# Fused sparse attention and MoE: the gate row through DRAM, ranks late in the pair, and four weight loads issued later

## The chip, the cores and the metric

The kernel runs on one core of one Trainium2 chip. The metric is the time of one execution on the device in microseconds (us). The kernel before takes 290.99 us, the median of three runs (290.3 to 291.02). Five engines work side by side, each through its own list of instructions in order: PE (TensorE, matrix products), DVE (VectorE), ACT (ScalarE), POOL (GpSimd) and SP (SyncE, which here only issues DMAs). They wait for each other through semaphores. POOL also issues DMAs, those of the weights and all indirect ones.

## The reference

The first half is attention with 4 batches, 8 heads, 768 positions and head size 64. Per query the keys' 24 chunks of 32 are bounded, the six best causal chunks are kept, and the softmax runs over those. Its output, written as 3072 rows x of 512, goes to a mixture of 8 experts with a capacity of 80:

```python
logits = x @ w_gate
expert_idx = np.argmax(logits, axis=1)
gate_w = probs[np.arange(N), expert_idx]          # probs: softmax of the logits
for e in range(E):
    tok_idx = np.where(expert_idx == e)[0]
    if len(tok_idx) > capacity:
        keep = np.argpartition(-gate_w[tok_idx], capacity)[:capacity]
        tok_idx = tok_idx[keep]
    h = np.maximum(x[tok_idx] @ w1[e], 0.0)
    out[tok_idx] = gate_w[tok_idx, None] * (h @ w2[e])
```

An expert keeps its 80 tokens with the largest gate weight; all other rows of the output are zero. So each token's rank inside its expert is needed before the experts can start.

## The kernel before, in words

**Attention.** The loop `for i in range(NP)` (L930) runs over 16 pairs of heads, four to a batch (`kk = i % 4` is the place in the batch). A pair does on PE, in order: scores of steps 0 and 1 (L509, with the chunk mask added by L524), the sums of the pair before (L581, L595), scores of steps 2 and 3, the transposes of the pair before's output rows (L641), scores of steps 4 and 5, the bounds of the next pair (L472), the values (L568), and the transposes of the next pair's unselected chunks (L497). ACT takes the exponentials (L531). POOL makes the causal selects on the diagonal blocks (L545) and adds the exponentials up into ES (the folds, L554), from which the sums are taken. DVE transposes q and k (L439, L449), reduces k to chunk minima and maxima (L453, L454) and picks the six best (L486).

**Ranking a batch.** While batch b is ranked, the pairs of batch b + 1 run (`bb = i // 4 - 1`). At kk = 0 the gate weights of 768 tokens are formed as `gt6`, 128 partitions by 6 tiles (`gate`, L678). They are also needed as a row on all partitions (`G`, columns S to 2S): `rank_row` (L713) makes it with six PE transposes and an ACT copy, and `rank_pred` (L720) writes a slightly smaller copy beside it, with which later tokens lose ties. Then 0/1 matrices are made that tell whose weight beats whose: `rank_own` and `rank_diag` for the diagonal blocks, and `rank_cmp` (L737), one compare of 640 columns for each of six tiles, rotated so that a tile's own block is left out. They lie in the space of weights that come later: tiles 0 to 4 in `w1s[7]`, tile 5 in `w2s[6]` (`Cs`, L303), and the program guards each of these two places as a whole, under the keys `w1_7` and `w2_6` (`Ck`). At kk = 2 `rank_count` (L783) sums them up per expert on PE, and `rank_slot`, `rank_hot`, `table` and `merge` place the tokens in their experts' lists. The last batch is ranked after the loop, by functions of its own (`last_row`, `last_diag`, `last_low`, `last_high`, `last_count`).

**Weights.** `wload(e, part)` (L414) issues from POOL one expert's W1 or W2, 1 MB each, one a pair in pairs 1 to 13; the last three follow in pair 15 (two before its selects). W1 of expert 6 has lent its space as the source of zeros for three of the four fills of the output. W2 of expert 7 has no place of its own: its eight quarters of 128 rows go into spaces that attention has left, with `last_w2` (L919), four in pair 15, and two each behind gathers 4 and 5 of the expert stage.

**Experts.** `gather(e)` (L1088) fetches 80 rows of x by index, `turn(e)` transposes them, `up(e)` multiplies by W1 and takes the relu (half on ACT, L1121, half on DVE, L1123), `down(r)` multiplies four groups of 32 tokens by W2, and a scatter (L1142) writes the rows out. Gathers, scatters and the late W2 loads stand in one order on POOL.

**Order.** There is no scheduler. Each engine's order is that of the program text. The class `Sync` (L18) puts the waits in: for each instruction the names it reads and writes are given, and it waits for the last writer of each, and a writer also for the last readers. A name given as read or written is waited for whether or not the bytes overlap.

Of the kernel before, what the change touches and what calls it, by code (L numbers as in the profile page):

```python
# [4 lines left out]
ALU = mybir.AluOpType  # L5
# [142 lines left out]
def bass_quest_chunk_select__then__topk_capacity_drop_kernel(  # L148
# [57 lines left out]
    with ExitStack() as pers:  # L206
# [13 lines left out]

        sy = Sync(nc)
        op = sy.op

        with nc.Block() as blk:

            @blk.sync
            def _body(_unused):
# [41 lines left out]
                gt6 = al(pers, "gt6", [128, NT])  # L269
# [40 lines left out]

                def T1v(b):
                    return bass.AP(w2s[E - 2], 0, [[FB * Dm, 128], [1, 2 * S]]).bitcast(F32)
# [77 lines left out]
                op("dve", lambda: ve.memset(wg[:], 0.0), w=["wg"])  # L390
                op("dve", lambda: ve.memset(onc[:], 0.0), w=["onc"])
# [286 lines left out]
                def gate(b):  # L678
                    op("dve", lambda: ve.scalar_tensor_tensor(oh[:], lg[:], 0.0, rank_c[:], ALU.is_ge, ALU.mult),
                       r=["lg", "rank_c"], w=["oh"])  # L680
                    op("dve", lambda: ve.tensor_reduce(lmax[:], oh[:], AX, ALU.max), r=["oh", "lmax"], w=["lmax"])
                    op("dve", lambda: ve.tensor_reduce(lsum[:], lgx[:], AX, ALU.add), r=["lgx", "lge"], w=["lsum"])
                    op("dve", lambda: ve.reciprocal(gt6[:], lsum[:]), r=["lsum"], w=["gt6"])
                    op("dve", lambda: ve.tensor_tensor(ohb[:, :, 0:E], oh[:], along(lmax), ALU.is_equal), r=["oh", "lmax"], w=["ohb"])

                def gate_digits(b):
                    op("dve", lambda: ve.tensor_copy(gsp[:, :, 0], gt6[:]), r=["gt6"], w=["gsp0"])
                    op("dve", lambda: ve.tensor_tensor(gdf[:], gt6[:], gsp[:, :, 0], ALU.subtract), r=["gt6", "gsp0"], w=["gdf"])
                    op("dve", lambda: ve.tensor_copy(gsp[:, :, 1], gdf[:]), r=["gdf"], w=["gsp1"])
                    op("dve", lambda: ve.tensor_tensor(gsp[:, :, 2], gdf[:], gsp[:, :, 1], ALU.subtract), r=["gdf", "gsp1"], w=["gsp2"])  # L690
# [11 lines left out]
                PRED = 1.0 - 2.0 ** -24  # L702

                def last_row():
                    for t in range(NT):
                        o = t * 128 if t < 3 else 128 + t * 128
                        gb = bass.AP(gt6, t, [[NT, 128], [0, 128]])
# [5 lines left out]
                def rank_row(b):  # L713
                    for t in range(NT):
                        gb = bass.AP(gt6, t, [[NT, 128], [0, 128]])
                        op("pe", lambda: pe.transpose(SC[1][:, ts(t)], gb, ident_f[:]),
                           r=["gt6", "ident_f"], w=["SC1"], inc=(t == NT - 1))
                    op("act", lambda: ac.activation(G[:, S:2 * S], SC[1][:, 0:S], ACTF.Copy), r=["SC1"], w=["grow"])

                def rank_pred():  # L720
                    op("act", lambda: ac.activation(G[:, 0:S], G[:, S:2 * S], ACTF.Copy, scale=PRED), r=["grow"], w=["growP"])

                def rank_own(b):
                    tq = bass.AP(triQ, 0, [[128, 128], [0, NT], [1, 128]])
                    gb = bass.AP(gt6, 0, [[NT, 128], [1, NT], [0, 128]])
                    op("dve", lambda: ve.tensor_tensor(T1v(b).rearrange("p (a b) -> p a b", a=NT), tq, gb, ALU.mult),
                       r=["triQ", "gt6"], w=["T1"] + Ck(b, NT - 1))

                def rank_diag(b):
                    for j0, n in ((NT - 1, 1), (0, NT - 1)):  # L730
                        o = Cs(b, j0, n, 0, 128)
                        a = T1v(b)[:, j0 * 128:(j0 + n) * 128].rearrange("p (a b) -> p a b", a=n)
                        g = G[:, S + j0 * 128:S + (j0 + n) * 128].rearrange("p (a b) -> p a b", a=n)
                        op("dve", lambda: ve.tensor_tensor(o, a, g, ALU.is_ge), r=["T1", "grow"] + Ck(b, NT - 1),
                           w=[f"D{jt}" for jt in range(j0, j0 + n)] + Ck(b, j0))

                def rank_cmp(b, *jts):  # L737
                    for jt in jts:
                        gj = gt6[:, jt:jt + 1]
                        o = Cs(b, jt, 1, 128, S - 128)[:, 0, :].rearrange("p (a b) -> p a b", a=NT - 1)  # L740
                        op("dve", lambda: ve.tensor_scalar(o, G[:, (jt + 1) * 128:(jt + 1) * 128 + S - 128], gj, None, ALU.is_lt),
                           r=["grow", "gt6"] + (["growP"] if jt < NT - 1 else []), w=[f"C{jt}"] + Ck(b, jt))

                def Cl(jt, lo, w):
                    t, o, row = (ES, jt, 2 * S) if jt < 4 else (vn[0], jt - 4, S)
                    return bass.AP(t, o * (S // 2), [[row, 128], [1, S // 2]]).bitcast(BF16)[:, lo:lo + w]

# [3 lines left out]
                def last_diag(*jts):  # L751
                    for jt in jts:
                        op("dve", lambda: ve.scalar_tensor_tensor(Cl(jt, jt * 128, 128), triQ[:], gt6[:, jt:jt + 1],
                                                                  G[:, S + jt * 128:S + (jt + 1) * 128], ALU.mult, ALU.is_ge),
                           r=["triQ", "gt6"] + gk(jt * 128, jt * 128 + 128), w=[f"D{jt}"])

                def last_low(jt, e):
                    n = jt * 128
                    o, x = Cl(jt, 0, n), G[:, S:S + n]
                    if e == "dve":  # L760
                        op("dve", lambda: ve.tensor_scalar(o, x, gt6[:, jt:jt + 1], None, ALU.is_lt), r=["gt6"] + gk(0, n), w=[f"L{jt}"])
# [4 lines left out]
                def last_high(jt):  # L766
                    n = (jt + 1) * 128
                    op("dve", lambda: ve.tensor_scalar(Cl(jt, n, S - n), G[:, S + n:2 * S], gt6[:, jt:jt + 1], None, ALU.is_le),
                       r=["gt6"] + gk(n, S), w=[f"U{jt}"])

                def last_count(order, warmth):
                    for n, jt in enumerate(order):
                        Cv = Cl(jt, 0, S).rearrange("p (t c i) -> p t c i", c=4, i=32)
                        for c in range(4):
                            op("pe", lambda: pe.matmul(MBf[c * 32:c * 32 + 32, 0:192], ohb[:, jt, :], Cv[:, :, c, :],
                                                       start=(n == 0), stop=(n == NT - 1)),
                               r=["ohb", f"D{jt}"] + ([f"L{jt}"] if jt else []) + ([f"U{jt}"] if jt < NT - 1 else []),
                               w=["MB"], inc=(n == NT - 1 and c == 3))
                        keep_warm(warmth[n])

                ORDER = [5, 4, 3, 2, 1, 0]

                def rank_count(b):  # L783
                    for n, jt in enumerate(ORDER):
                        for lo, hi, o in ((0, NT - jt, jt), (NT - jt, NT, 0)):
                            if lo == hi:
                                continue
                            Cv = Cs(b, jt, 1, lo * 128, (hi - lo) * 128)[:, 0, :].rearrange("p (t c i) -> p t c i", c=4, i=32)
                            last = jt == ORDER[-1]
                            for c in range(4):  # L790
                                op("pe", lambda: pe.matmul(MBf[c * 32:c * 32 + 32, o * 32:(o + hi - lo) * 32], ohb[:, jt, :], Cv[:, :, c, :],
                                                           start=(n == 0 and lo == 0), stop=last),
                                   r=["ohb", f"C{jt}", f"D{jt}"] + Ck(b, jt), w=["MB"], inc=(last and c == 3))
# [136 lines left out]
                for i in range(NP):  # L930
# [10 lines left out]
                    if i == NP - 1:  # L941
                        wload(E - 2, 1)
# [6 lines left out]
                    if live and kk == 1:  # L949
                        rank_pred()  # L950
                        rank_cmp(bb, 5)
# [6 lines left out]
                    if live and kk == 2:  # L958
                        rank_count(bb)
# [15 lines left out]
                    if live and kk == 0:  # L975
                        gate_exp()
                        gate(bb)
                    scores(i, 4, 6)
# [9 lines left out]
                    if i == 3:  # L988
                        op("dve", lambda: ve.tensor_scalar(triM[:], triQ[:], 1.0, 3e38, ALU.is_ge, ALU.mult), r=["triQ"], w=["triM"])
                        op("dve", lambda: ve.scalar_tensor_tensor(triM[:], ident_f[:], 3e38, triM[:], ALU.mult, ALU.max),  # L990
                           r=["triM", "ident_f"], w=["triM"])
                    if i + 4 < NP:
                        load(i + 4, "qk")
                    if i == NP - 4:
                        load_vk(NP - 1, 0)
                    if live and kk == 0:
                        rank_own(bb)
                    if live and kk == 1:
                        rank_diag(bb)
                        rank_cmp(bb, 4, 3, 2, 1, 0)  # L1000
# [17 lines left out]
                    if live and kk == 0:  # L1018
                        rank_row(bb)
# [3 lines left out]
                    if 0 < i < NP - 2:  # L1023
                        wload((i - 1) // 2, (i - 1) % 2)
                    if i in (0, 1, 12):
# [20 lines left out]
                last_high(0)  # L1046
                last_low(5, "act")
                values_out(1)
                last_low(4, "act")
                last_low(3, "act")  # L1050
                last_diag(0, 1, 2, 3, 4, 5)
                last_low(1, "dve")
                last_high(1)
                rows(NP - 1)
                keep_warm(4)
                last_high(4)
                last_high(3)
                last_low(2, "dve")
                last_high(2)
                scale_rows(NP - 1)  # L1060
                gate_gcols(b)
                last_count((0, 5, 1, 4, 2, 3), (0, 0, 0, 0, 0, 6))
# [96 lines left out]
                last_w2((4, 5))  # L1159
                for e in range(1, E):  # L1160
                    if 1 < e + 1 < E:
                        turn(e + 1)
                        if e + 4 < E:
                            gather(e + 4)
                            if e == 1:
                                last_w2((6, 7))
# [41 lines left out]
```

## Time and profile before

The page shows one profiled execution. It took 292.94 us itself, of which the span from the first to the last instruction is 291.1 us.

| | us | share of the span |
|---|---|---|
| PE busy | 275.7 | 95% |
| POOL busy | 226.5 | 78% |
| DVE busy | 213.7 | 73% |
| ACT busy | 147.0 | 51% |
| fold adds on POOL, L554, 135 of them | 148.3 | 51% |
| compares of 640 columns, L741, 18 of them | 15.5 | 5% |
| gate-row transposes on PE, L716, 18 of them | 2.5 | 1% |
| mean granted TensorE clock | 0.988 of full | |

Busy times overlap, as the engines run side by side. The chain of waits, followed back from the last instruction, is 65% PE, 19% POOL and 7% DVE. A pair has no marker of its own; its start can be read from the five transposes L497 and the first score matmul L509 behind them. Loop bodies of one kind recur 16 times with nearly the same durations, so that a pair which differs stands out.

### The profile page before, as it was taken

To read this page: it belongs to the slowest core of one execution; us is meant where nothing else is said; L and a number is where in the kernel's file an instruction comes from. 1 tells how busy PE (TensorE), PEld (TensorE's weight loads), DVE (VectorE), ACT (ScalarE), POOL (GpSimd) and SP (SyncE) were. 2 spreads that over 40 slices of the span, in tenths; PEclk is the share of its full clock that TensorE was granted. 3 is DMA by queue.
4 is the path that set the end of the run, shared out by engine and by line. 5 is a ranking of instruction groups with operands and counts; after the bars stand their busy time and mean duration, and the time that the engine had idled before them with its cause. 6 is when DMAs were issued, how large, how long until landed. Compare 5 with 4: busy or idle time off the path is not lost.

```text
span 291.1 us, 8693 instructions
## 1 busy us (share of the span) xinstructions
PE 275.7 (95%) x3606; PEld 169.9 (58%) x3609; DVE 213.7 (73%) x575; ACT 147.0 (51%) x202; POOL 226.5 (78%) x295
## 2 busy tenths in 40 slices
PE   7998999999999999999999999999998999885991
PEld 7554656565656565656564657565655675453661
DVE  5897555566978988759889888898899798811341
ACT  2275655555666454645655555656656554321320
POOL 6079899998999999989999999899969950075232
PEclk9999999999999999999999999999999999998997
DMA  9988999999999999999999979999999799416111
GB/s 149 178 141 142 295 173 204 256 173 168 179 159 167 166 184 170 173 153 187 155 168 155 180 136 188 158 187 171 188 315 148 263 148 196 75 55 128 39 59 60
DMA packets 158359, 47.95 MB, mean 165 GB/s; under 512 B 142405, under 2 KB 150721, under 8 KB 158320
## 3 DMA queue, kind: packets, MB, share of 16 engines
q1 hardware_dynamic: 141664, 28.34, 50.2%
q0 software_dynamic: 13520, 18.67, 40.1%
q10 hardware_dynamic: 3136, 0.39, 0.9%
q8 instruction: 28, 0.46, 0.6%
q14 instruction: 11, 0.09, 0.1%
HBM read 53.49 MB, written 11.01 MB: 222 GB/s over the span
## 4 chain that ended last, share of the span: by engine, by line
PE 65%; POOL 19%; DVE 7%; DMA 3%; issue 3%; ACTq 1%; POOLq 0%; ACT 0%; DVEq 0%
PE SC L509 20%; PE OB L568 18%; POOL ES L554 14%; PE SC L524 4%; PE OB L1136 3%; PE M L595 3%; POOL EXB L545 3%; PE OB L641 3%; PE SC L1112 2%; PE M L472 2%; PE M L581 2%; PE MB L497 2%; DMA qn<-in_q_dram 1%; DMA unsT<-in_moe_w_dram 1%; DMA qn<-x_rows,idx 1%
## 5 line engine op out<-in xcount | busy, mean ns | idle before, releaser
L531 ACT ACTIVATE EXB<-SC 128x1024 f32<-128x1024 f32 x96 | 86.3, 917 | 46.4 <-PE SC L524 45.1
L554 POOL TENSOR_TENSOR ES<-ES,EXB 128x256 f32<-128x256 f32 (+1 forms) x105 | 101.7, 980 | 4.8
L509 PE MATMUL SC<-qT,kT 64*128 64x512 f32 (+3 forms) x512 | 96.3, 466 | 0.1
L568 PE MATMUL OB<-EXB,vn 128*64 128x256 f32 (+3 forms) x704 | 73.0, 361 | 2.1 <-POOL EXB L545 2.1
L568 PEld LDWEIGHTS OB<-EXB,vn 128*64 128x64 f32 x704 | 46.8, 137 | 25.6 <-issue 9.8
L509 PEld LDWEIGHTS SC<-qT,kT 64*128 64x128 f32 x512 | 41.4, 186 | 23.0 <-issue 14.3
L554 POOL TENSOR_TENSOR ES<-EXB 128x768 f32<-128x768 f32 (+1 forms) x30 | 46.6, 1554 | 2.5
L524 PE MATMUL SC<-unsT,ind 64*128 64x128 bf16 (+5 forms) x256 | 37.7, 289 | 0.1
L576 ACT ACTIVATE oT<-OB 128x512 f32<-128x512 f32 (+1 forms) x32 | 15.6, 489 | 40.0 <-PE OB L568 40.0
L545 POOL TENSOR_SCALAR_AFFINE_SELECT EXB<-EXB 128x256 f32<-128x256 f32 x79 | 33.8, 437 | 0.5 <-ACT EXB L531 0.5
L524 PEld LDWEIGHTS SC<-unsT,ind 64*128 64x128 bf16 x256 | 12.8, 95 | 17.8 <-issue 8.0
L439 DVE STREAM_TRANSPOSE qT<-qn 128x768 f32<-128x768 f32 x16 | 15.6, 974 | 7.2 <-PE SC L524 6.4
L586 DVE STREAM_TRANSPOSE M<-M 128x192 f32<-128x192 f32 x16 | 6.3, 395 | 19.6 <-PE M L595 19.3
L661 DVE TENSOR_TENSOR xp<-OB,rden 128x768 bf16<-128x768 f32 x16 | 15.3, 954 | 6.6 <-PE OB L641 6.3
L443 ACT ACTIVATE rq<-qT 128x768 f32<-128x768 f32 x16 | 13.5, 843 | 9.7 <-DVE qT L439 9.1
L1089 POOL DMA_INDIRECT qn<-x_rows,idx x4 | 4.0, 993 | 17.7 <-DVE idR L1080 16.7
L1142 POOL DMA_INDIRECT out_dram<-EXB,idR x6 | 6.0, 998 | 14.6 <-DVE EXB L1140 8.9
L449 DVE STREAM_TRANSPOSE kT<-kn 128x768 f32<-128x768 f32 x16 | 15.5, 966 | 1.3 <-DMA kn<-in_k_dram 1.3
L453 DVE TENSOR_REDUCE kmm<-kT 128x24 f32<-128x768 f32 x16 | 15.2, 950 | 0.5
L454 DVE TENSOR_REDUCE kmx<-kT 128x24 f32<-128x768 f32 x16 | 15.1, 943 | 0.0
L486 DVE MAX8 top<-M 128x8 f32<-128x8 f32 (+4 forms) x160 | 14.6, 165 | 0.6
L641 PE MATMUL OB<-ident_f,oT 128*128 128x128 f32 x96 | 13.9, 281 | 0.5 <-ACT oT L576 0.5
(222 smaller groups left out, 418.7 us busy)
## 6 DMA issues: line engine op xcount, KB each, us to landing
w1s<-in_moe_w_dram POOLq DMA_DIRECT2D x8, 1024.0 KB, 10.1
w2s<-in_moe_w_dram POOLq DMA_DIRECT2D x7, 1024.0 KB, 10.8
vn<-in_v_dram SPq DMA_DIRECT2D x32, 192.0 KB, 3.3
kn<-in_k_dram SPq DMA_DIRECT2D x62, 96.0 KB, 3.0
qn<-in_q_dram SPq DMA_DIRECT2D x62, 96.0 KB, 4.0
out_dram<-w1s SPq DMA_DIRECT2D x3, 1536.0 KB, 7.9
x_rows<-xp SPq DMA_DIRECT2D x16, 192.0 KB, 3.5
out_dram<-G SPq DMA_DIRECT2D x1, 1536.0 KB, 10.7
```

Source lines behind the costliest of these rows:

```text
L439: op("dve", lambda: ve.transpose(qT[j][:], qn[s][:].rearrange("p a b c -> p (a b c)")), r=[f"qn{s}{g}" for g in range(4)], w=[f"qT{j}"])
L449: op("dve", lambda: ve.transpose(kT[j][:], kn[s][:].rearrange("p a b c -> p (a b c)")), r=[f"kn{s}{g}" for g in range(4)], w=[f"kT{j}"])
L453: op("dve", lambda: ve.tensor_reduce(kmm[j][:, 0, 0:NCH], kv, AX, ALU.min), r=[f"kT{j}"], w=[f"kmm{j}"])
L509: op("pe", lambda: pe.matmul(o, kT[j][pr, ts(kt)], qT[j][pr, q0:q1], start=True, stop=False), r=[f"kT{j}", f"qT{j}"], w=[f"SC{s}"], inc=False)
L524: op("pe", lambda: pe.matmul(o, ind[pr, ts(kt)], unsT[j][pr, b0 - 128:q1 - 128], start=False, stop=True), r=[f"ind{h}", f"unsT{j}"], w=[f" ...
L531: op("act", lambda: ac.activation(Ex(st, None, 0, W), src, ACTF.Exp, scale=SCALE), r=[f"SC{s}"], w=[f"E{st}"])
L545: op("gp", lambda: gp.affine_select(ad, a, pattern=[[0, 2], [1, 128]], compare_op=ALU.is_ge, fill=0.0, base=0, channel_multiplier=-1), r=[ ...
L554: op("gp", lambda: gp.tensor_tensor(o, in0, in1, ALU.add), r=[f"E{s2}", f"E{first[0]}"] if first else [f"E{s2}"] + kt, w=kt)
L568: op("pe", lambda: pe.matmul(OB[pr, q0:q1], vn[s][:, kt, h, :], ex, start=(n == 0), stop=last), r=[f"vn{s}{h}", "ES0" if st is None else f ...
L576: op("act", lambda: ac.activation(oT[:, q0:q1], OB[:, q0:q1], ACTF.Copy), r=[f"O{bk}"], w=[f"oT{bk}"])
L641: op("pe", lambda: pe.transpose(OB[:, ts(t)], oT[:, ts(t)], ident_f[:]), r=["oT0", "oT1", "ident_f"], w=[f"O{t // 4}"], inc=(t in (3, NT - ...
L661: op("dve", lambda: ve.tensor_tensor(xo, xi, rx, ALU.mult), r=["O0", "O1", "rden"], w=[f"xp{i % 2}"])
```

## The change

It has five parts.

- `rank_row` and `rank_pred` go. In their place `row_out` transposes `gt6`, padded to 32 columns, in 32 x 32 blocks on DVE and writes it to a small DRAM buffer from SP, and `row_in` reads it back to all 128 partitions. Both are at kk = 0.
- The 0/1 matrices are no longer rotated: a tile's columns are the 768 tokens in order. The functions of the last batch (`diag`, `low`, `high`, `count`) now serve all four batches; in place of one compare a tile there are a diagonal block and one compare to each side of it.
- For batches 0 to 2 all of these stand at kk = 1 behind `take_k`, where before one compare stood earlier in the pair and the first products at the end of kk = 0.
- W1 of expert 6 is no longer issued at the end of pair 13, nor W2 of expert 6 in pair 15: both are issued at the end of pair 14.
- The last four quarters of expert 7's W2 are issued behind gather 7.

```diff
+                def row_out():
+                    op("dve", lambda: ve.transpose(gtT[:], gt6[:]), r=["gt6"], w=["gtT"])
+                    o = bass.AP(gd.tensor, gd.offset, [[32, 4], [128, 32], [1, 32]])
+                    op("sp", lambda: sp.dma_start(o, gtT[:]), r=["gtT"], w=["gd"], dsem="d_gd")
+                def row_in():
+                    a = bass.AP(gd.tensor, gd.offset, [[0, 128], [1, S]])
+                    op("sp", lambda: sp.dma_start(G[:, S:2 * S], a), r=["gd"], w=["grow", "growA", "growB"], dsem="d_gr")
...
+                def Cw(b, jt):
+                    return Ck(b, jt) if b < B - 1 else []
+                def diag(b, *jts):
                     for jt in jts:
+                        op("dve", lambda: ve.scalar_tensor_tensor(Cl(b, jt, jt * 128, 128), triQ[:], gt6[:, jt:jt + 1],
                                                                   G[:, S + jt * 128:S + (jt + 1) * 128], ALU.mult, ALU.is_ge),
+                           r=["triQ", "gt6"] + gk(jt * 128, jt * 128 + 128), w=[f"D{jt}"] + Cw(b, jt))
+                def low(b, jt, e="dve"):
...
+                        op("dve", lambda: ve.tensor_scalar(o, x, gt6[:, jt:jt + 1], None, ALU.is_lt), r=["gt6"] + gk(0, n), w=[f"L{jt}"] + Cw(b, jt))
+                def high(b, jt):
...
+                    op("dve", lambda: ve.tensor_scalar(Cl(b, jt, n, S - n), G[:, S + n:2 * S], gt6[:, jt:jt + 1], None, ALU.is_le),
+                       r=["gt6"] + gk(n, S), w=[f"U{jt}"] + Cw(b, jt))
+                def count(b, order, warmth=(0,) * 6):
...
                     if i == NP - 1:
-                        wload(E - 2, 1)
                         wload(E - 1, 0)
                     folds(i, 0, 1)
...
-                    if live and kk == 1:
-                        rank_pred()
-                        rank_cmp(bb, 5)
                     scores(i, 2, 4)
...
                     if live and kk == 2:
-                        rank_count(bb)
+                        count(bb, (5, 0, 4, 1, 3, 2))
                         rank_slot(bb)
...
                     if live and kk == 0:
                         gate_exp()
                         gate(bb)
+                        row_out()
...
+                    if live and kk == 0:
+                        row_in()
...
-                    if live and kk == 0:
-                        rank_own(bb)
                     if live and kk == 1:
-                        rank_diag(bb)
-                        rank_cmp(bb, 4, 3, 2, 1, 0)
+                        diag(bb, *range(NT))
+                        for jt in (5, 0, 4, 1, 3, 2):
+                            if jt:
+                                low(bb, jt)
+                            if jt < NT - 1:
+                                high(bb, jt)
...
-                    if live and kk == 0:
-                        rank_row(bb)
...
-                    if 0 < i < NP - 2:
+                    if 0 < i < NP - 3:
                         wload((i - 1) // 2, (i - 1) % 2)
+                    if i == NP - 2:
+                        wload(E - 2, 0)
+                        wload(E - 2, 1)
...
                 gather(4)
-                last_w2((4, 5))
...
                         if e + 4 < E:
                             gather(e + 4)
-                            if e == 1:
-                                last_w2((6, 7))
+                            if e + 4 == E - 1:
+                                last_w2(range(4, FB))
```

## The prediction, before the changed kernel had run

> **What bounds the kernel now.** I read the page's shares first (PE 95% busy, POOL 78%, DVE 73%), then the chain that ended last, because shares don't say which of three busy engines sets the pace. The chain in order of time (start us, us, what):
>
> ```profile
> 54.42 1.06 PE SC L509 x4
> ...
> 68.34 1.06 PE SC L509 x4
> ...
> 74.05 0.81 PE OB L641 x6
> ...
> 82.25 0.66 PE SC L716 x6
> 82.91 1.06 PE SC L509 x4
> ...
> 102.80 0.64 PE MB L791 x44
> ...
> 111.64 1.06 PE SC L509 x4
> ```
>
> A head pair on whose way only TensorE lies takes 68.34 - 54.42 = 13.92 us. The pairs that also rank a batch take longer: from the unselect transposes (L497) of one pair to the next, pair 5 has 14.58 (0.66 is the gate-row transposes, L716), pair 6 14.81 (0.64 is the counting, L791), pair 7 14.15. Batches 0 and 1 agree to 0.02. Pair 14 takes 16.55. Next the timeline of VectorE and GpSimd around a ranking (start us, us, engine, instruction, [idle before <-releaser]); the fourth line is from pair 15, where GpSimd is idle:
>
> ```profile
> 203.08 1.81 POOL L554 TENSOR_TENSOR ES<-EXB 128x768 f32<-128x768 f32 x1
> 203.21 2.04 DVE L741 TENSOR_SCALAR w2s<-G,gt 128x640 bf16<-128x640 f32 x1
> 204.85 0.66 POOL L545 TENSOR_SCALAR_AFFINE_SELECT EXB<-EXB 128x256 f32<-128x256 f32 x1
> 245.61 0.55 DVE L768 TENSOR_SCALAR ES<-G,gt 128x640 bf16<-128x640 f32 x1
> ```
> ```profile
> 98.98 3.30 DVE L741 TENSOR_SCALAR w1s<-G,gt 128x640 bf16<-128x640 f32 x5
> ...
> 102.73 0.12 PEld L791 LDWEIGHTS MB<-w2s,ohb 128*32 128x32 bf16 x8 [0.32 <-DVE M L586]
> ```
>
> A compare that takes 0.55 took 2.04 because a fold add of 1.81 was running: it ended 0.35 after the add. And the counting on PE starts when VectorE's compares are over (102.28): that wait is already at zero slack. Last, the tail, and the granted clock after its gap (columns: PE, PEld, DVE, ACT, POOL, clock, DMA share, GB/s):
>
> ```profile
> 217.92 0.79 POOL L417 DMA_DIRECT2D w1s<-in_moe_w_dram  x1 [2.14 <-DMA out_dram<-w1s]
> ...
> 267.04 0.44 ACT L1121 ACTIVATE kT<-SC 128x320 bf16<-128x320 f32 x1 [3.63 <-DMA unsT<-in_moe_w_dram]
> ```
> ```profile
> 264.20:267.40 3.20, 0.20 (x2) 0.00 (x0) 0.40 (x1) 0.36 (x1) 2.28 (x3) 0.94 0.82 174
> 267.40:268.40 1.00, 0.87 (x12) 0.34 (x16) 0.00 (x0) 0.07 (x1) 0.00 (x0) 0.50 0.33 81
> ```
>
> ScalarE's relu of expert 2 writes kT0, which the late W2 loads are recorded as reading, so it waits until the last of them has landed; PE then runs at half clock until 270.44.
>
> [...] the 2.04 above, L990 (scalar_tensor_tensor, two SBUF inputs) 0.829 beside an add against 0.346 for L753 with GpSimd idle, and 0.28 to 0.55 for 128 to 640 elements, 1.9 a ns. [...] here it was 0.50 for 3.4 us after 3.2 us of idleness. [...] here x_rows landed in 11.7 us among weight loads and in 2.4 without.
>
> **The change part by part**, against the profiled 292.94 us (span 291.1; the median of the runs is 290.99, 1.95 less).
>
> 1. *Gate row.* Gone from PE: 6 transposes, 0.66, three times: -2.0. Gone from ScalarE: L718 0.81 and L721 0.83; from VectorE in mid-pair: L726 1.40 and the 2.04. These sit off the chain, except that they make GpSimd late: pair 6's excess of 0.89 is 0.64 of counting and 0.25 of waiting for L554; I drop 0.25 in pairs 6 and 10: -0.5. New: a 128x32 VectorE transpose (0.40 for 192 columns, 0.32 for 160: some 0.2), before L439, which idles 0.65 for PE anyway; two DMAs. A landing for 8 KB is 3.3 us, for the 384 KB broadcast I take 4: 8 us, with the whole next pair (13.9) before its reader. SP stands in row_in's wait some 3 us; behind it are the loads of pair i+4, whose reader is two pairs away. Cost 0; uncovered 8 once a batch. The new memset, 0.07, start-up.
>
> 2. *Ranks late in the pair.* Before, VectorE's late chunk was 2 diagonal ops and 5 compares, 96.81 to 102.28. Now it is 6 scalar_tensor_tensor (0.346) and 10 tensor_scalar, two each of 128 to 640 elements (0.28, 0.35, 0.42, 0.48, 0.55): 2.08 + 4.16, and 15 gaps of 0.036 as between the L741s: 6.8 us alone. It starts where it did, with the last k reduce, at the next pair's start P (68.32 against 68.34 in pair 4), and isn't alone: GpSimd has two to three adds left (to P+1.9), its wload, two selects from P+3.6 (released by the sums), then adds of 1.81, 1.27 and 1.28 with selects between. I walk the two queues[...]. Diagonals 0 to 2 end at 0.6, 1.3, 2.1, all six at 3.2; low 5, high 0, low 4 at 3.8, 4.4, 5.0; high 4 sits behind the 1.81 add to 6.7; low 1 7.2; high 1 behind the 1.27 to 8.6; low 3 9.1; high 3 behind the 1.28 to 10.4; low 2 10.8; high 2 11.2. Shifting the adds by 0.3 or the gaps to 0.1 gives 11.1 to 11.7; if one compare slips ahead of an add, about 10. I take 10.9.
>  PE reaches the counting at P+5.7 (where L641 stands in a plain pair, 74.05 - 68.34). Its second tile waits on key w1_7, whose last writer is the last compare, so the new order of tiles doesn't help. PE waits 5.2 us a batch: +15.6. Behind it on PE queue the rows, scores 4 and 5, bounds and values; behind the chunk on VectorE the sums' transposes, rden, scale_lg (1.2) and rank_slot, done before PE needs M0 and OB again. GpSimd runs out of folds. The counting itself is 24 matmuls of 192 columns in place of 44 shorter ones: the same columns, 0.64. Bounds of the wait: 1.1 (no blocking: 6.8) and 6.
>  A gap of 5 us is longer than the one of the tail, where 32 matmuls then took 3.24 against 1.9. I take 1.2 a batch: +3.6 (0 to 5).
>
> 3. *W1 and W2 of expert 6 behind pair 14's folds.* Pair 14's excess of 2.63 is 0.64 counting, 0.40 table and 1.6 GpSimd's wait for the zero fill and the issue: -1.6. Two issues (0.79, 0.91) now stand before pair 15's selects, which GpSimd reaches earlier, having waited for PE: 0; without that cover 0.8. But 1 MB more goes through the weight queue late: pair 15's packets move some 180 KB/us, so 5.7 us more. They ended at 250; relative to pair 15 I get some 4 later, past the issue of the last x_rows (250.3), which every gather waits for. A third of its 11.7 in company, the rest alone: +2.0 (0 to 5).
>
> 4. *The last W2 quarters behind the last gather.* The relu's wait of 3.6 goes, and the half clock with it: down(1) would end at 264.0 + 1.9 = 265.9, not 270.8: -4.8. Next on the chain is turn(4), whose gather (259.84 + 2.7) is in; gather 7 no longer waits behind two more issues. The four loads land about 5 us after gather 7, some 4 before down(5) reads them. Least gain 3.1.
>
> Sum: -2.0 - 0.5 + 15.6 + 3.6 - 1.6 + 2.0 - 4.8 = +12.3: profiled 305.2, median 303.3.
>
> **The rivals.**
> *The compares run beside the folds* (ends on the other side). If scalar_tensor_tensor and tensor_scalar aren't held, the chunk ends at P+6.8, PE waits 1.1, no half clock: -6.9 + 3.3 = -3.6: 287.4. It decides at a wait of 2.3, a chunk end at P+8.0. For it: four of the five L741 at 98.98 ran at 0.55 to 0.57 beside a DMA issue and selects. Against: the four L741 or L990 cases above, and that after 5 us no such GpSimd gap is left.
> *The late weights own the DMA engines* until x_rows and the gathers are some 6 late: 307 to 308. For it: 11.7 us for pair 14's x_rows. Against: x_rows of pair 15 found the queue empty.
> *The tail's wait only changes its name* (gather 4 or the scatter's place in GpSimd's order): part 4 gives nothing, 308. For it: GpSimd has 1.0 a gather, one after the other. Against: gathers 3 and 4 were issued before 261.
>
> **How the numbers follow.** Main case 0.68, own range 298 to 308 (no half clock and no DMA delay 297.7; wait 5.8, full half clock 308). First rival 0.15, second 0.10, third 0.07. Forecast 303. The range 294 to 309 holds the main case and the second and third rival but for a few hundredths, some 0.83. Within 0.3% is what a measurement here can't tell from no change. Slower: 0.68 + 0.17 = 0.85; of the rival's 0.15, 0.02 fall within.
>
> **What would show it.** Right: single compares of about 1.7, 1.4 and 1.3 on VectorE in pairs 6, 10 and 14 beside L554; PE idle some 5 us before the second tile of the counting, released by VectorE; clock 0.50 behind it; pairs 5, 9 and 13 at 13.92; no wait of ScalarE for a weight load after 255; the first gather 1 to 3 us later after pair 15's start. Wrong: compares of 0.3 to 0.55 throughout, or a gap on PE under 2.3 us.

## The result and the profile after

The changed kernel takes 308.06 us (median of four runs, 307.4 to 310.72), the kernel before 290.64 beside it (289.68 to 291.02): ratio 1.0622, 95% interval 1.0553 to 1.0691. The profiled execution took 307.83 us, its span is 306.1 (before 292.94 and 291.1). In the experiments below the kernel before measured 294.08, 292.11 and 292.59 beside the three groups of runs, so ratios are to that group's own. Some executions are slower as a whole, and a ratio compares only the others, so that it isn't always the quotient of the two medians and is missing where too few were left.

The chain of waits of the changed kernel, around the first ranking (start us, us, what):

```profile
82.23 1.06 PE SC L510 x4
...
101.09 1.73 DVE w1s L750
103.19 1.52 DVE w1s L750
105.22 1.26 DVE w1s L750
107.36 0.99 PE MB L757 x16
```

The chain of before came to the counting of this pair through GpSimd's adds, the sums and the scores on PE, without VectorE:

```profile
98.34 1.20 POOL ES L554
99.54 0.04 issue
99.58 0.86 PE M L595 x16
...
102.80 0.64 PE MB L791 x44
```

Now the chain leaves PE and GpSimd and follows VectorE through three long compares. The timeline of the changed kernel at this place, GpSimd, VectorE and PE together:

```profile
100.86 1.86 POOL L555 TENSOR_TENSOR ES<-EXB 128x768 f32<-128x768 f32 x1
101.09 1.72 DVE L750 TENSOR_SCALAR w1s<-G,gt 128x128 bf16<-128x128 f32 x1
103.16 1.26 POOL L555 TENSOR_TENSOR ES<-ES,EXB 128x512 f32<-128x512 f32 x1
103.19 1.51 DVE L750 TENSOR_SCALAR w1s<-G,gt 128x512 bf16<-128x512 f32 x1
105.05 1.26 POOL L555 TENSOR_TENSOR ES<-EXB 128x512 f32<-128x512 f32 x1
105.22 1.25 DVE L750 TENSOR_SCALAR w1s<-G,gt 128x256 bf16<-128x256 f32 x1
...
107.36 0.99 PE L757 MATMUL MB<-w1s,ohb 128*32 128x192 bf16 x20 [5.31 <-DVE w1s L750]
```

Each long compare begins while an add runs and ends 0.09, 0.28 and 0.16 us behind it. PE stands idle for 5.31 us in front of the second tile of the counting, and the 20 matmuls behind the gap take 0.99 where 0.64 was expected for the whole counting. The windows behind the gap of pair 6, and in and behind that of pair 10 (PE, PEld, DVE, ACT, POOL, clock, DMA share, GB/s):

```profile
107.36:110.75 3.39, 3.39 (x30) 2.41 (x32) 2.44 (x7) 0.00 (x0) 0.00 (x0) 0.50 0.62 100
...
168.78:170.89 2.11, 0.00 (x0) 0.00 (x1) 2.04 (x4) 0.00 (x0) 1.06 (x1) 0.50 1.23 198
170.89:175.60 4.71, 4.71 (x40) 3.23 (x40) 2.50 (x7) 0.00 (x0) 0.00 (x0) 0.50 0.46 102
```

The clock is 0.50 for 3.41 us in pair 6, and for 6.83 us each in pairs 10 and 14. Last, the tail in the timeline:

```profile
283.48 0.44 ACT L1091 ACTIVATE kT<-SC 128x320 bf16<-128x320 f32 x1
...
289.81 0.63 POOL L890 DMA_DIRECT2D rq<-in_moe_w_dram  x1
```

ScalarE's relu of expert 2, which had waited 3.63 us for the late weights, waits for nothing now; the loads go out 6 us after it.

Where the time went, from one set of unselect transposes to the next (us):

| | before | changed | difference |
|---|---|---|---|
| pairs 5, 9, 13 | 14.58, 14.58, 14.57 | 13.92 each | -1.97 |
| pair 6 | 14.81 | 21.55 | +6.74 |
| pair 10 | 14.81 | 22.20 | +7.39 |
| pair 14 | 16.55 | 22.35 | +5.80 |
| pair 15's transposes to gather 0 | 25.42 | 26.39 | +0.97 |
| gather 0 to the end | 36.94 | 33.08 | -3.86 |

With 0.05 less in the other pairs that is +15.0, the difference of the two spans.

### The profile page after: what moved, and what is told of

It is laid out like the page before. It is cut to its first block, busy times and chain, and to the rows that moved or that the text cites. A ratio compares the mean times of both kernels' runs of the same rounds, so it can differ in the third digit from the quotient of the medians.

```text
span 306.1 us, 8565 instructions
## 1 busy us (share of the span) xinstructions
PE 276.5 (90%) x3531; PEld 170.5 (56%) x3531; DVE 217.5 (71%) x600; ACT 142.5 (47%) x196; POOL 221.5 (72%) x295
## 4 chain that ended last, share of the span: by engine, by line
PE 69%; DVE 21%; POOL 3%; DMA 2%; issue 2%; ACTq 1%; POOLq 0%; DVEq 0%
PE SC L510 22%; PE OB L569 19%; DVE w1s L750 5%; PE OB L642 4%; PE SC L525 4%; PE OB L1106 3%; PE SC L1082 3%; DVE w1s L735 3%; PE M L596 3%; PE M L473 2%; PE M L582 2%; DVE w1s L743 2%; DVE kmm L454 2%; PE MB L498 1%; DVE qT L440 1%
## 5 line engine op out<-in xcount | busy, mean ns | idle before, releaser
L555 POOL TENSOR_TENSOR ES<-ES,EXB 128x256 f32<-128x256 f32 (+1 forms) x105 | 100.2, 966 | 4.8
L510 PE MATMUL SC<-qT,kT 64*128 64x512 f32 (+3 forms) x512 | 98.7, 476 | 0.1
L510 PEld LDWEIGHTS SC<-qT,kT 64*128 64x128 f32 x512 | 42.7, 192 | 23.0 <-issue 16.7
L577 ACT ACTIVATE oT<-OB 128x512 f32<-128x512 f32 (+1 forms) x32 | 15.6, 489 | 38.5 <-PE OB L569 38.5
L757 PE MATMUL MB<-w1s,ohb 128*32 128x192 bf16 x60 | 3.0, 362 | 15.9 <-DVE w1s L750 15.9
L750 DVE TENSOR_SCALAR w1s<-G,gt 128x640 bf16<-128x640 f32 (+4 forms) x15 | 16.8, 1117 | 0.4
L642 PE MATMUL OB<-ident_f,oT 128*128 128x128 f32 x96 | 15.9, 309 | 0.5 <-ACT oT L577 0.5
## 6 DMA issues: line engine op xcount, KB each, us to landing
out_dram<-w1s SPq DMA_DIRECT2D x3, 1536.0 KB, 12.3
```

The lines of the kernel that those rows point to most:

```text
L510: op("pe", lambda: pe.matmul(o, kT[j][pr, ts(kt)], qT[j][pr, q0:q1], start=True, stop=False), r=[f"kT{j}", f"qT{j}"], w=[f"SC{s}"], inc=False)
L555: op("gp", lambda: gp.tensor_tensor(o, in0, in1, ALU.add), r=[f"E{s2}", f"E{first[0]}"] if first else [f"E{s2}"] + kt, w=kt)
L577: op("act", lambda: ac.activation(oT[:, q0:q1], OB[:, q0:q1], ACTF.Copy), r=[f"O{bk}"], w=[f"oT{bk}"])
L642: op("pe", lambda: pe.transpose(OB[:, ts(t)], oT[:, ts(t)], ident_f[:]), r=["oT0", "oT1", "ident_f"], w=[f"O{t // 4}"], inc=(t in (3, NT - ...
L750: op("dve", lambda: ve.tensor_scalar(Cl(b, jt, n, S - n), G[:, S + n:2 * S], gt6[:, jt:jt + 1], None, ALU.is_le), r=["gt6"] + gk(n, S), w= ...
```

## The experiments

The theory to be tested is that of the prediction: a compare of VectorE that meets one of GpSimd's adds ends only behind it (by 0.09 to 0.28 us in the timeline above), the chunk of 16 instructions ends 11 us into the pair, PE waits for it, and pays again through the clock (0.50 behind the gap). The rivals are that the compares are long by themselves, that the guard on the whole place w1_7 makes the wait, that only the counting's place is wrong, or that the row through DRAM and the late weights have a share.

### Each part alone

The parts are numbered as in the prediction: 1 the row, 2 the ranks (columns and place), 3 the weights of expert 6, 4 the tail.

Only the tail:

```diff
-                last_w2((4, 5))
...
-                            if e == 1:
-                                last_w2((6, 7))
+                            if e + 4 == E - 1:
+                                last_w2(range(4, FB))
```

> The kernel before with only the last four quarters of expert 7's W2 moved behind gather 7. Held theory (part 4 takes a wait off the end): ScalarE's relu of expert 2 no longer waits 3.6 us for a weight load, the half clock behind it goes; the stretch from gather 0 to the end shrinks from 36.96 by 3.1 to 4.8 us as it did in the changed kernel (33.08, though gather 1 landed 1 us late there). Median 286.0 to 287.5. Since the profiled execution of before lay 1.95 over its median, the gain on the median may be 2 us smaller, 288.5, if that difference sits in this wait. Rival (the wait only changes its name): 290.6, another wait of 3 to 4 us in its place.

Measured: 290.04 against 294.08, ratio 0.9884 (0.9774 to 0.9994). No wait for a weight load in the tail; gather 0 to the end 34.35 in this execution. A second run of the same kernel:

> The kernel before with only the last W2 quarters behind gather 7, once more beside the next three. Held theory: ratio 0.985 to 0.990 to the kernel before, no wait of ScalarE for a weight load in the tail, end 34.3 after gather 0. Rival (the first measurement was one of luck): 1.00.

Measured: median 290.7 (287.95 to 292.98) against 292.59, no ratio. Gather 0 to the end is 32.00 in the profiled one (287.95). So the wait did go and no other took its place; what it is worth differs from one execution to the next, 2.6 to 4.9 us against the 36.94 of the first profile.

Only the weights of expert 6:

```diff
                     if i == NP - 1:
-                        wload(E - 2, 1)
                         wload(E - 1, 0)
...
-                    if 0 < i < NP - 2:
+                    if 0 < i < NP - 3:
                         wload((i - 1) // 2, (i - 1) % 2)
+                    if i == NP - 2:
+                        wload(E - 2, 0)
+                        wload(E - 2, 1)
```

> The kernel before with only W1 and W2 of expert 6 moved to the end of pair 14. Held theory: pair 14 falls from 16.55 to 14.96 (-1.6); the weight queue drains some 3 us later relative to pair 15's start (P15 + 23 in place of P15 + 20), which costs the end nothing beyond 1 us of late instruction fetch or late x_rows: 289.0 to 290.0. Rival (the late weights own the DMA engines and hold x_rows and the gathers back by 6): 295.

Measured: 294.27, ratio 1.0041 (1.0014 to 1.0068): a small loss. Pair 14 takes 15.06, but gather 0 comes 28.15 after pair 15's transposes in place of 25.42. In the chain of waits:

```profile
249.25 5.69 DMA x_rows<-xp
```

The last rows of x land 5.69 us after their issue, 2.4 before. That is the predicted delay; the stretch to gather 0 grew by 2.7 us.

Only the row through DRAM:

```diff
+                        row_out()
...
+                    if live and kk == 0:
+                        row_in()
...
-                    if live and kk == 0:
-                        rank_row(bb)
```

> The kernel before with only the gate row taken through DRAM (row_out, row_in), the rotated 0/1 matrices and their places kept, the ACT copy with the smaller weights kept too. Held theory: pairs 5, 9 and 13 fall from 14.58 to 13.92 (-2.0), pairs 6 and 10 by up to 0.25 (-0.5); the two DMAs are hidden: 288.2. Rival (the row lands too late for the early compare in mid-pair, or SP's wait holds up the loads behind it): 290.6 or more, with a wait for gate_row on VectorE or ScalarE.

Measured: 301.98 against 294.08, no ratio. Three of the four executions took 301.93 to 302.55, the fourth 297.03; the profile is of one of the three. In it pairs 9 and 13 take 13.92 as expected, but pair 5 takes 23.26. In the timeline:

```profile
83.84 0.65 SPq L720 DMA_DIRECT2D gate_row<-gtT  x1
86.55 0.34 SPq L724 DMA_DIRECT2D G<-gate_row  x1
...
94.57 0.84 ACT L727 ACTIVATE G<-G 128x768 f32<-128x768 f32 x1 [9.05 <-DMA G<-gate_row]
```

VectorE had the row ready at 78.08. SP, standing behind key loads that wait for their buffers, wrote it out at 83.84; the broadcast issued at 86.55 landed 7.99 us later (the median of this execution's three is 3.8); and ScalarE, which reads it in mid-pair in the old place of the ranks, held the exponentials for 9.05 us. PE ran at half clock for 6.83 of the pair. The rival was right for this batch of this execution; the fourth execution, 5 us shorter, has no profile.

Only the ranks (the changed kernel with parts 3 and 4 undone by the reverse of the diffs above, and the row made by PE transposes again):

```diff
-                        row_out()
...
-                    if live and kk == 0:
-                        row_in()
...
+                    if live and kk == 0:
+                        rank_row(bb)
```

> The changed kernel with the row made by six PE transposes and an ACT copy as before, and the weights and the tail as before: only the unrotated 0/1 matrices, all behind take_k. Held theory (the whole loss is here): VectorE's chunk ends 11.2 us after its pair's start, PE waits 5.3 us in pairs 6, 10 and 14 and runs at half clock behind it; 308.1 + 2.5 + 0.6 + 2 to 4 for what the other three parts had given: 313 to 315. Rival (some of the 18 us in these three pairs belongs to the row through DRAM or to the late weights): under 308, with a PE gap under 4 us.

Measured: 317.68, ratio 1.0834 (1.0744 to 1.0925), some 24 us over its group. Pairs 6, 10 and 14 take 21.68, 21.94 and 21.96, nearly as in the changed kernel, and the chunk ends 11.28, 11.27 and 11.44 us after the pair's start. The loss in these pairs belongs to the ranks alone; neither the row nor the weights have a share that can be seen. No run takes the second part apart: before, the late chunk was 7 instructions and ended 5.5 us after the pair's start (102.28), now it is 16, and how much of the loss is the number of instructions and how much their place isn't shown. The total is 2.7 to 4.7 higher than expected; the kernel before of this group is itself 3.4 over the one from which the estimate was made. In the tail the relu waits 3.8 us for the weights, and the clock halves for 6.83 (40.15 us from gather 0 to the end).

### What makes the chunk long

The adds of the three pairs left out:

```diff
-                        for (s2, c2, q0, q1) in ADDS[st] if i < NP - 1 else []:
+                        for (s2, c2, q0, q1) in ADDS[st] if i < NP - 1 and i not in (6, 10, 14) else []:
```

> The changed kernel with GpSimd's fold adds left out in pairs 6, 10 and 14, so the softmax sums of these pairs are incomplete; nothing else is touched. Held theory (VectorE's compares are long[...]): all compares at 0.28 to 0.55, the chunk ends 6.6 to 7.0 us after its pair's start in place of 11.2, PE waits 1.0 to 1.3 in place of 5.3, no half clock behind it; each of the three pairs falls by about 6: 308.1 - 18 = 290. Rival (the compares are as long by themselves, from their shapes or places): chunk and total as in the changed kernel, 308.

Measured: 296.39, ratio 1.0164 (1.0141 to 1.0187), in place of 1.0622. Pairs 6, 10 and 14 fall to 19.18, 16.73 and 18.55, by 11.6 in all and not by the 18 expected. Pair 10 in the timeline:

```profile
162.40 0.29 DVE L750 TENSOR_SCALAR w1s<-G,gt 128x128 bf16<-128x128 f32 x1
...
163.05 0.48 DVE L750 TENSOR_SCALAR w1s<-G,gt 128x512 bf16<-128x512 f32 x1
...
164.04 0.35 DVE L750 TENSOR_SCALAR w1s<-G,gt 128x256 bf16<-128x256 f32 x1
...
165.38 0.60 PE L757 MATMUL MB<-w1s,ohb 128*32 128x192 bf16 x20 [2.02 <-DVE w1s L750]
```

The same three compares that took 1.71, 1.51 and 1.25 now take 0.29, 0.48 and 0.35: 3.35 us less. The chunk ends at 7.95 and not at 11.23. It doesn't come down to 6.6 to 7.0, since the adds of the pair before still run when it starts: three diagonal blocks take 0.45, 0.77 and 0.77 in both kernels, the others 0.35. So PE's wait is 2.02, not 1.0 to 1.3. In pair 6 the chunk also waited 1.28 for its row, which had been under way since 84.80, and PE waited 2.87; and the clock halved for 3.41 in pairs 6 and 14, where no half clock was expected (mean clock 0.983). These waits and the clock make up the 6 us above the 290 expected. That the adds make the compares long is shown; the rival is out. By what means they do so isn't shown.

The guard made finer, so that five tiles wait only for their own compares:

```diff
-                               r=["ohb", f"D{jt}"] + ([f"L{jt}"] if jt else []) + ([f"U{jt}"] if jt < NT - 1 else []) + Cw(b, jt),
+                               r=["ohb", f"D{jt}"] + ([f"L{jt}"] if jt else []) + ([f"U{jt}"] if jt < NT - 1 else []) + (Cw(b, 5) + Cw(b, 0) if n == NT - 1 else []),
```

> The changed kernel with the counting of the first five tiles waiting only for the tile's own compares; only the sixth still waits for the whole place w1_7. Held theory (the last compare sets the end of the wait, the key costs the counting of four tiles at most): PE's long gap is cut into pieces, the counting ends at most 0.7 us earlier a batch; 306 to 308. Rival (the key on the whole place makes the wait): the gap goes, 292 to 295.

Measured: 308.6, ratio 1.0575 (1.0551 to 1.0599). PE in the timeline of pair 6:

```profile
103.12 0.27 PE L757 MATMUL MB<-w1s,ohb 128*32 128x192 bf16 x4 [0.73 <-DVE w1s L750]
105.03 0.27 PE L757 MATMUL MB<-w1s,ohb 128*32 128x192 bf16 x4 [1.64 <-DVE w1s L750]
106.78 0.35 PE L757 MATMUL MB<-w1s,ohb 128*32 128x192 bf16 x4 [1.49 <-DVE w1s L750]
107.63 0.35 PE L757 MATMUL MB<-w1s,ohb 128*32 128x192 bf16 x4 [0.49 <-DVE w1s L750]
```

One gap of 5.31 has become four of 4.35 together. The last tile still starts 11.3 us after the pair's start, so that the counting ends only some 0.6 earlier, as expected; but the clock now halves for 6.83 in all three pairs, in pair 6 too (mean clock 0.961, in the changed kernel 0.971), and they take 21.95, 22.40 and 22.44. The guard makes at most a small part of the wait, and nothing is gained without it.

The counting moved to between the two halves of the values, with the ranks' use behind it:

```diff
-                    if live and kk == 2:
-                        count(bb, (5, 0, 4, 1, 3, 2))
-                        rank_slot(bb)
...
                         bounds_out(i + 1)
+                    if live and kk == 2:
+                        values(i, (0,))
+                        count(bb, (5, 0, 4, 1, 3, 2))
+                        rank_slot(bb)
```

> The changed kernel with the counting (and the ranks' use) moved from before the rows to between the two halves of the values, 5 us later on PE, so that the chunk is over when PE gets there. Held theory (the chunk blocks VectorE's queue, not only the counting): PE then waits in front of the next pair's bounds, whose bank is free only when the sums' transposes, behind the chunk, have read it: 4.2 to 4.9 us in place of 5.3, total 305 to 308. Rival (only the counting's place costs): the gap goes, 290 to 293.

Measured: 306.52, ratio 1.0508 (1.0429 to 1.0587). In the timeline PE now waits here:

```profile
108.76 0.47 PE L473 MATMUL M<-qT,kmm 64*32 64x160 f32 x1 [4.28 <-DVE lgp L652]
```

The bounds need a bank that the sums' transposes and the product L652 must have read, and these stand behind the chunk on VectorE. So the counting is only the first of the things that the chunk holds up; moving it takes 1 us off PE's wait and does not free it.

### What the gap costs twice

PE kept busy while it waits:

```diff
-                        keep_warm(warmth[n])
+                        if b < B - 1 and n == 0:
+                            keep_warm(24, OB, "O0")
+                        else:
+                            keep_warm(warmth[n])
```

> The changed kernel with 24 matmuls of 512 columns of no use (about 5.1 us of PE) put behind the first tile of the counting, so that PE isn't idle while it waits. Held theory (the gap costs twice, by itself and by the half clock behind it): the chunk and the counting's start stay where they are, the clock stays at 1.00, pairs 6, 10 and 14 fall to 19.9, 19.9 and 20.3 us (by 1.7, 2.3 and 2.1): 302. Rival (what I booked to the clock is other waiting behind the chunk): 308.

Measured: 301.84, ratio 1.0346 (1.0316 to 1.0376). PE in the timeline, and the window behind the gap:

```profile
102.28 5.13 PE L857 MATMUL OB<-ind,ident_bf 128*128 128x512 bf16 x23 [0.16 <-issue]
107.45 0.60 PE L757 MATMUL MB<-w1s,ohb 128*32 128x192 bf16 x20
```
```profile
107.45:110.75 3.30, 3.30 (x68) 2.46 (x76) 2.57 (x8) 0.55 (x1) 0.00 (x0) 1.00 1.01 197
```

The counting starts 11.31 us after the pair's start, as without the useless matmuls, and takes 0.60. The clock stays at 1.00 until the last 3.5 us of the kernel. Pairs 6, 10 and 14 take 20.05, 20.05 and 20.30. So the half clock costs 1.50, 2.15 and 2.05 us in the changed kernel, 5.7 in all.

### Without the second part, and a second look at before

The changed kernel with the ranks as before, which is the kernel before with the three diffs of the tail, the weights and the row:

> The changed kernel without its second part: row through DRAM from SP, weights and tail as changed, the ranks rotated and placed as in the kernel before. Held theory (the ranks' place alone costs the 16 us and the clock): PE gap before the counting 0.3 to 0.6, no half clock there; if the row lands in time ratio 0.985 to 0.995, and 1.01 to 1.025 where the first batch's row lands 8 us late as it did with the row alone. Rival (row and weights cost as much together as the ranks): ratio over 1.04.

Measured: 297.22, ratio 1.0203 (1.0107 to 1.0300). The counting waits for nothing long (pair 6 takes 14.56, pair 14 15.50). What is left is a row that came late in pair 5 (18.96; ScalarE waits 4.8 for it) and x_rows behind the weights (28.24 to gather 0). Some 4 points of the 6.2% go with the second part; the other three together do not win either.

The row issued from ScalarE's queue, with the tail's edit kept. The diff shows the queue alone, against the kernel with the row alone; the write also stands later there, behind `take_r`, and the broadcast between the two halves of the values:

```diff
-                    op("sp", lambda: sp.dma_start(o, gtT[:]), r=["gtT"], w=["gd"], dsem="d_gd")
+                    op("acd", lambda: ac.dma_start(o, gtT[:]), r=["gtT"], w=["gd"], dsem="d_gd")
...
-                    op("sp", lambda: sp.dma_start(G[:, S:2 * S], a), r=["gd"], w=["grow"], dsem="d_gr")
+                    op("acd", lambda: ac.dma_start(G[:, S:2 * S], a), r=["gd"], w=["grow"], dsem="d_gr")
```

> The kernel before with the tail's loads behind gather 7 and the gate row through DRAM, both DMAs issued from ScalarE's queue, which gets to them earlier than SP's, whose loads stand in front. Ranks and their places as before. Held theory (the row was late in the kernel with the row alone because SP's queue was late and a weight load then went first): pairs 5, 9 and 13 at 13.9, pairs 6 and 10 at 14.6, no wait for gate_row over 1 us; 2 us less than the kernel with the tail alone: ratio 0.980. Rival (a landing is late with any queue while weights move): a wait for gate_row of 3 to 9 us in pair 5, ratio 1.00 to 1.02.

Measured: 292.38 against 292.59 (287.43 to 294.11), no ratio. The waits in its profile:

```profile
POOL w1s L421 <- DMA out_dram<-w1s: 4.0, 1, 4.0
...
ACT G L729 <- DMA G<-gate_row: 2.4, 3, 1.1
```

The row is in time but for 1.1 us at most, and pairs 5, 9 and 13 take 13.92, 14.08 and 13.92. Pair 6 takes 15.10 and pair 10 14.94 in place of 14.81, so the waits give back some of it. In the profiled execution GpSimd also waited 4.0 for a fill of zeros in pair 14, and the clock halved behind it (mean clock 0.984), which made that pair 21.42. A gain over the tail alone isn't shown.

The kernel before once more:

> The kernel before, unchanged, for a second profile. Held theory (pair 14's wait of 2.1 us for the fill of zeros in the first profile was that execution's own, since it was 0.1 to 0.6 in two kernels that issue the load at the same place): pair 14 at 15.1 to 15.5 in place of 16.55, so part 3 had 0 to 0.4 to remove. Rival (the wait is there in every execution): 16.5.

Measured: ratio 1.0005 (0.9984 to 1.0026), profiled execution 294.24. Pair 14 takes 15.09, with no wait for the fill. But pair 10 takes 18.92 where it took 14.81: PE waited 2.23 for a load of v, and the clock halved for 3.41 behind it. The tail's wait is there:

```profile
ACT kT L1121 <- DMA unsT<-in_moe_w_dram: 3.5, 1, 3.5
```

but the clock stays at 1.00 behind it, and gather 0 to the end takes 35.50, not 36.94. With the same code up to pair 14, four executions have 16.55 and 15.09 (before) and 15.07 and 16.51 (tail alone): the pair's wait comes and goes by 1.5 us. (In the last one the profile puts GpSimd's 2.0 before its weight load down to PE, not to the fill.)

## Why the prediction was right or wrong

The direction held, and so did the way to it: long compares beside the adds, PE's wait, half clock behind it. 308.06 lies inside the range of 294 to 309, just at the top of the main case's own 298 to 308, and 5 us above the forecast of 303. (That 308 does not come out of the two terms named for it: a wait of 5.8 and 5 us of half clock give 306.5.) By the steps:

1. **Gate row.** -2.0 was forecast for PE, -1.97 measured. The 0 for the two DMAs was right for the changed kernel, because its readers come at the end of the next pair. The size was wrong for the first batch: the way through DRAM was put at 8 us and began, in the forecast, when the row was ready. Measured from that moment it took 10.9, 5.5 and 5.3 us in the changed kernel, and 16.5 in the first batch with the row alone. The step named the loads behind the row on SP, but not those in front of it.
2. **Ranks late in the pair.** Chunk end forecast at 10.9 (the walk gave 11.2), measured 11.23, 11.24 and 11.24; the 14 ends of the walk through the two queues, an estimate of the author's from the lengths of the adds and compares, are met within 0.12 us in pair 6; compares of 1.7, 1.4 and 1.3 forecast, 1.72, 1.51 and 1.25 measured; PE's wait 15.6 forecast, 15.9 measured, in front of the second tile, released by VectorE. Leaving the adds out shows the cause. The statement that the new order of tiles doesn't help was right, but for another reason than the forecast gave: without the guard on w1_7, named there, PE's wait is still 4.35, because the last tile needs the last compare.
   **The half clock** was mis-sized: 3.6 forecast, 5.7 measured. The forecast scaled one stretch of the tail, and two of three gaps were followed by twice that stretch.
3. **Weights of expert 6.** The -1.6 holds against that one profile only. It was read as a standing wait, and the second profile of before and one of the tail alone don't have it; against those the part gives nothing. The +2.0 for x_rows was right in kind: 2.7 with the weights alone. In the changed kernel x_rows was itself later and landed before gather 0 needed it; there the stretch grew by 0.97 by another way, of which 0.75 is a pause of PE that the profile gives no releaser for. The kernel with the ranks only, whose weights are as before, has a pause of 1.10 in the same stretch, so the weights alone don't explain it. Its cause is open.
4. **Tail.** -4.8 forecast, -3.9 measured against the profiled execution of before, of which a late landing of gather 2 takes back about 1 (3.97 us from its issue to the copy of its transposed rows, 2.92 before). Against the second profile of before the gain is 2.4.

**The sum.** Against before's profiled execution +12.3 was forecast and +14.9 measured (307.83 - 292.94): 2.1 more for the clock, 0.9 for the tail and 0.3 for PE's wait, 1.0 less at x_rows; the remaining 0.3 is about what was booked too much for GpSimd's waits in pairs 6 and 10. Of the 5.06 us to the median, 2.6 are this, and 2.2 lie in the last step, from the profiled execution to the median. The forecast took 1.95 off for both kernels alike. But that execution of before had a wait in pair 14 (1.5 us) and a half clock in the tail (36.94 - 35.50 = 1.4) that another execution did not have, and the change takes both away; the changed kernel's own profiled execution lies 0.23 under its median. Counting -1.6 and the clock's part of -4.8 as gains, and subtracting 1.95 as well, probably took the same microseconds twice; the median execution of before has no profile that could show it.

**The rivals.** The first (compares run beside the folds) fell: none of the kernels with adds shows it. The second (late weights hold the gathers 6 late) exists at 2.7 and 2.8 in two kernels and not at all in the changed one; that its 307 to 308 is close to the result is chance. The third (the tail's wait changes its name) fell with the tail alone.

The only edit with a measured gain is the fourth part on its own: ratio 0.9884 (0.9774 to 0.9994). The interval nearly reaches 1, and the second measurement could not confirm the size.

## What to carry to other kernels

In these kernels a run of compares on VectorE costs its own time only where GpSimd has no adds: three that took 1.71, 1.51 and 1.25 us beside the adds took 0.29, 0.48 and 0.35 with them left out. Beside a chain of adds, see in the timeline which compare meets an add (here of 1.26 to 1.86 us) and count to the end of that add, then ask what else stands behind the run in VectorE's queue, since moving the first reader only moved the wait (5.31 us before the counting, 4.28 before the bounds). A transfer that is taken off an engine and sent through DRAM needs its cover counted from when the data are ready (5.3 to 16.5 us for the row), with all that stands in front of it on the issuing queue. And before a wait in one profile is priced as a gain, look whether a second execution has it.

## What was not expected of the hardware

- In the trace of the changed kernel the clock was at 0.50 from 107.34 to 110.75 (3.41 us), and for twice as long from 168.78 to 175.60 and from 233.63 to 240.46. In pair 6 that began at the end of a gap of 5.31, in pair 10 2.1 us before the end of an equal gap. With the adds left out a gap of 2.02 was followed by no half clock in pair 10 and by 3.41 us of it in pair 14: the four score matmuls L510 of 64x384 behind it take 0.92 and 1.65.
- In the changed kernel PE was without a matmul for 3.41, 3.19 and 2.98 of the 3.41 us before 107.34, 168.78 and 233.63. Of the first 3.41 at half clock behind each it was idle for 0.02, 2.11 and 2.33, and behind the last two of these a second 3.41 at half clock followed. In the kernel before it was idle for 2.62 of the 3.41 before the half clock at 267.03. The 3.41 from 100.51 in the changed kernel, with 1.86 of idleness, were followed by full clock. By what rule the clock changes isn't shown.
- The way of a row of 768 numbers through DRAM to 128 partitions varied a good deal: the broadcast alone landed in 3.3 us (the changed kernel) to 9.5 us (the counting moved) over these kernels, and with the adds left out 7.5 us passed between the issue of the first write and that of its read, against 2.8 in the changed kernel.
